# A new order table for a fused decay attention and gated MLP, with reciprocal transfers also issued by ScalarE

## The chip, the cores and the metric

The kernel runs on one core of a Trainium2 chip. The time is device microseconds of one execution. The core has TensorE (PE in the profile; PEld is its weight load), VectorE (DVE), ScalarE (ACT), GpSimd (POOL) and SyncE (SP), which here does nothing but issue transfers; each works through its own queue in order, and semaphores tie them together.

## What is computed

Inputs are q, k, v of 8 batches x 8 heads x 576 x 64, a forget factor f per position, a value weight and an output weight of 512 x 512, and a convolution weight of 5 x 512. Per head:

```python
scores = q @ k.T / sqrt(64)
cum = cumsum(log(clip(f, 1e-4, 1)))
scores = where(causal, scores + cum[i] - cum[j], -1e9)
attn = softmax(scores)          # sum + 1e-9 below the line
x = attn @ v
```

Then the heads of a batch are put side by side (x is 576 x 512) and

```python
gate = sigmoid(sum over k of conv_w[k] * x[s - 4 + k])
out = (gate * (x @ w_val)) @ w_out
```

## The kernel before

**Tiling.** Two heads make a pair; there are 32 pairs, four to a batch. Of a pair, TensorE computes scores in nine blocks (`plan_s`, class S; two pairs of heads, four row blocks and a joint tail). DVE adds the decay from a table in SBUF and finds the row maximum (line 479, class red), ScalarE takes the exponential with a row sum (line 483, class SX, tiles P and Pl). TensorE transposes the result (`plan_pt`, class PT, line 511) and ScalarE or DVE evicts the transposed blocks from PSUM to tile pt (line 268, class PE in the plan). TensorE multiplies with v (`plan_pv`, class PV), and DVE multiplies the product by the reciprocal of the row sums while evicting it (line 580, class X, tile x). The result is split into two fp32r halves, xh and its remainder xl (line 587), and is convolved: five products along the sequence, the first a plain product (line 273 on ScalarE, 275 on DVE or POOL), the other four on DVE (line 616); ScalarE's tanh makes the gate (line 592). After the fourth pair of a batch `plan_moe` computes x @ w_val (Mv), the gated product on DVE (line 648, H), its split (hh, hl) and the output product (Mo), whose eviction (ScalarE line 689, DVE line 691) halves it and whose store goes out in rows of 128. Pairs from the fifth on have their q and k split likewise into Xh and Xl (line 397 is Xl).

**The round trip of the reciprocals.** Row sums stand one per partition, but the product of PV needs them along the free dimension. So `rec` takes the reciprocals, TensorE transposes them with the last block (lines 529 and 530), they are copied to tile rt (line 532), written to DRAM with two transfers (class rzw, tile rzd, about 4.5 KB) and read back with two transfers that spread each row over 64 partitions of x32 (class rzr, 144 KB each). Line 580 uses them in place. A read may be issued when both writes have landed.

**Order.** Nothing is scheduled on the chip. The program first collects 2,712 pieces of work as nodes (`Plan.add`; `Plan.dma` adds a second node for the landing), each with the engines that may do it, what it reads and writes, and the PSUM banks that it is the first to touch. Then `Plan.order` reads TABLE: two characters give a node's number in base 64, a digit its engine (0 TensorE, 1 ScalarE, 2 DVE, 3 POOL, 4 SP), and a further digit each bank that it takes. Each engine gets its instructions in the order of the table; the table was found by a search outside the kernel. `load` makes a transfer; with `early=True` the table may give it to SP or ScalarE, otherwise only to SP. In the old table all transfers are on SP.

The issue itself is one line for all transfers (line 280):

```python
lambda e: (nc.sync if e == "SP" else nc.scalar).dma_start(out=out, in_=in_)
```

Of the kernel before, what the change touches and what calls it, by code (L numbers as in the profile page):

```python
# [47 lines left out]
423M15A41s21u14z21t24F24D23R003S11v35I37z44A14G14B24E14H0177t43A21y13x001z24M24C13y23D31A24-
023T034Y054143B13U13P063_44I21H45y449004U034Z11B24O23C31C14J14N13Q24K27v41D24L14P13E25_051E24T24t41G34a21S447016027K17L3482540475g24V15h25525845H31F15
647I13F26117B45e14d15f14W004X17J34b14c35S0135X21K24_11J15V25J046755T250025U15Z25118O45K25L18I48Q45O25P15Q252005R15a44e25M21M25c41L25313G25N11N11O27x45  # L50
Y15k077F382045W17H3832a345-16223H28X16b018Z38411P21Q11R37V0027G38-25l263036c16416f0646r18K46g15E46q26j46h4a147-
26p15i056s19X48W365071U18Y2670321468169015j25m21V29h047_15o16618026a17W27Y27X11X29i2bi47Z16l44f25n36d061W26e19j16n41Y18e008U3980734g2ba49d24h27M014651
Z28116v027R28f1aa1ab39e1ac1ad37S17T27U17N28M47O17P26t008c05992a938d17Q19Z47D48a0686018b28V39a16w21-
22038528716u26I05a7388068915p26x18i0278s18u1bg48v25q26y28j18m48_001649021_18g028t2942bo38k43I16J09119f26F076G09g19_46K2bp2bq3a839629518q4aw058h19719b2
9c19p029q18o46H26L1br1ax2ay1di48w049225r28y00231do45s29318x2an0724i1bc45t1ae06513as28z2ao29l009m1at16N04aq2af29k26z16O0aj28S4al2am1ah26M3ag16Q006R09n0
39t06ai1ap1bs3ex4au26S2dk4ak1dz36P2av19r056T2dq49u1be49s1242dA36V006W06U29o1dx3ar16Y046Z08C16A26B29x0179I1dw36X26-
29v056_18D29y19z49B49F49K1aI066C22629w1aE00aF19D4bL029H16D29L04aJ1bt065079J1bM2bN1bn3az2bC013bA26E1271bm3by2bz19N02bk4aA00bB1bH2bu2bv1bD2aG078A1bw2740
6aH1bx1dy3dm4bI1bE1aB2750a548E2aK00aL1aM075bF2703bP01bQ1aN1bJ2bK1ez4du37100720aZ19O2eF42522829M2bG1aQ4762aO4aS4292eM1aX2dT018B2dU2aC04aW1dV1aY12b3bT05
aU4bU1fM4aD27906732dv38F2dK034dL2dR2dB00521eD4dP2b0079P1dC2dM1dQ1eN3dI2dD1a-
03dJ1772bO2b_001783dE2dF1dG2bZ05dH1b12ca1cc1bV07bW19R3bX02dN2fO4eB4c022a1e301bR07c34a_2b43e41fU4fS4f-3dS1bS19S2g12cb1dX03b-  # L60
2c917a08G27b28H17e057f0b21c147c49T2c747j007k0eK3c54dY2eO1bY19Q2eP2f606eL3g239U2fY3b52eJ37g2b62cd03f_1f72dO1h74cf027l2eH4ds4f81cg2ce2b32ch1eZ045f42dW2c
i3eQ01620eT2f51g_4d_07e01eU1e-2cs03g03cj1e_1f02eX2h14cp07cq0ct0eY17h4eV2eW1f22cr2f31e7060b72eh1ej2j249V2h54e502e81e61fi04fj2f11hd3b82eR2dZ07cx06cy0d-
1eS1ck2cl27o02fQ4fZ3e94hg1hh3eb4ef4ed47p0gl04cA07cB0ei1e101ek2cu2fe00cv1cm2cn27q29W17r4en03gm2cw2gn1e21el04cC2cz2cD1b91fW4gc056em2ff1he1gf2gg1hf3kh4g3
02170jh1eo2fa04cE3fb1cF03gh2gd2gj27m4gk1hb3ga2gb1cG0cI04cJ0g42g51g62gi1cQ06jj3g82g91f92fm072ji3h34gp00cH2g71cK2ja4ge1fn2fc04fo4fz1fx2gq2fd1co1cL1fq4cM
3fk05fl2fw1gt01gu1fy2j44er2cR0hA03fs4cN02go2hB2kn4hC1hi00157cS2hc3hj2hr034fu4hl2fg06ky3fh1hm1hk1es2kw1hp2hn2hs2ho1hy2cO0fA06cP2cT2fC00ht1h94hu2fD2gB01
2gC1fB2gF4hw2gr05cU2hx1cV00gD4cW0gO2fG1kz2hq1kp4gx07hv1fE1gL2gN1fH2jk3gH4gM1cX2hM03c-
06c_0hz1et2eu2gs1fI2hD2ev2d02hO00gy1gz01gv04ep1gJ4hE02j84hN2gw1eq3gA1hI07hJ1hK06hG05hF2lw4kx2jg2jD03jE2gP07jF1hL2gR01gQ2hP1je3hH1fJ2gS2gV1j64ju024jv2e
w1jz2jA1jl06370kv3jw1jf3jB2cY4i201jm2hQ025kj4jc4kt3lE4jq2jn1d306d40kl4h_1js2jx2i12hR2jC1jy1fF2jo2kS04gT2jt1gW2lL3jr1d800jp1gX2hU4lN1kT2d90d51kU1jG2gU2
jP07jQ2i01h-
1i402hS4d14lC4hY4jT074jN05hW4i32i52i61i82jU2k32da1lK3k41ly4lO3k11k21mL4jO1kr4lM3m502m62fK2m71jV4kJ016kO2kK2oT4i73kA00475kP1mT4ku3kH2jL03kI1n03lI3jX4kQ  # L70
2kR1jZ4ie02if0j_4kF2kG1jM2d64ih05jJ07jK1mR4kM2kN1ig2kD2jH03gY2fL1jR02mN4db4ii0kB2kC1jS2kE1m-
2m_2dd07de0ij2jI1k503k700df1gZ2kL1kV2l6041li1mZ2n13lA4kW06lJ3l405l51mX3k-
02k_1lh1ik2il2i92ia2lj1k82lg1ip07l72l84la4ib2k62kb1iq0ir2nk00nl2oZ4ic2l005kY02o_4k91nm1lG4im07qe4qc4in0kX1kc2lP04301io2kZ1l12kd2lY067l205iu02iv0g-
1lS2lQ2lR1is2q64lU2m32m41dg4m12l32lZ2ix04iy0lV1lT1lW2lk05lm00m21lX1mf01it3l_2iz2m01iw2l-
1mh02p81p93le4ke2iA2m82mP4ml036mY3iB3mg1mb07lc4ka2m901mi1mv1mw2mj04mk1mm1mn4mp4mx2ln2ll2lo2lp3iC02iD0iF04id1iE2ma2mc1p61nb032p72my1n201675nc2lq1lr2md0
0me1n72ng2p52qn3n92mt4na1iG0iH2iP00ql3iI2iJ3n81ni2n32n41n52n61nd1nh1mr4ps04pt2mz07ne2pu1kf2kg1qm3mA2mB01mC2mD1no03mF2np2iQ0qo3oV4ls2mG2p33pj015po2nf1p
a06743iR1nj1rl4rC3nn2q84pk2rA1pf2nq00nr1iK02pb2pg1oX4nA040lt2nB2p43ph2mE3iL0nN1pc1mV4nC4qa4pl1pp1nL1iU06pd2nM1nw00pe1iM2pA01pm2iN4nK1nu02pq2mH2ns07pr1
pn1iS4lu2pi1nE4qj3sA4lv1rt4iV0qi3mI2rn4qk2pB1qH04qI2nx1qJ1py03nv1pv2nI4pw01nG4px2nt1rB3nQ00iW2mJ2pI021pz1pJ1ny04pK4pU1pS1pV2qp05376qu2pT1qy021mK1nz1sR
# [742 lines left out]
```

## Time and profile before

| | us |
|---|---|
| runs shown | 524.27, 532.27, 534.39 |
| their median | 532.27 |
| the profiled execution | 527.19 |
| its span, first to last instruction | 525.3 |

The profile is of one execution. Busy times are sums of the time in which an engine had an instruction in flight; for TensorE the ends are modelled and neighbours overlap. "Idle before" is the time that an engine stood before an instruction, put down to what came last. L253 is a helper that issues all products but the transposes, and L268 one that makes all copies, so there the tiles tell what it is: banks<-pt,vt is PV, banks<-xh,wall is Mv, banks<-wall,hh is Mo. P and Pl are what the exponentials write; "ACT P L483" as a releaser is that exponential. The clock was granted in full (the column PEclk, 1.00).

### The profile page before, as it was taken

Reading aid. Unit: us, or ns where it says so; the run is one execution under the profiler, and the core shown is the slowest. Engines: PE = TensorE matmul, PEld = TensorE weight load, DVE = VectorE, ACT = ScalarE, POOL = GpSimd, SP = SyncE. Lnnn points to the kernel's source line nnn. Section 1 sums busy time; section 2 is a strip of 40 time slices with the busy share of each in tenths; the row PEclk is TensorE's granted clock in tenths of the full one; section 3 lists DMA queues with packets and bytes.
Section 4 is the critical chain, followed back from the end, with each engine's and each line's share of the span. In section 5 each row is a group of like instructions: output and inputs, shape, how many; then the busy total and the mean of one; then the engine's idle time right before and its main releaser. Section 6 shows DMA issues by size and latency. Waiting matters only on the chain. (4 is left out here: it accounts for less than half of the span.)

```text
span 525.3 us, 12611 instructions
## 1 busy us (share of the span) xinstructions
PE 504.5 (96%) x4392; PEld 443.6 (84%) x4392; DVE 438.7 (84%) x1186; ACT 347.6 (66%) x991; POOL 224.3 (43%) x293
## 2 busy tenths in 40 slices
...
GB/s 212 307 237 325 282 282 288 187 225 157 224 214 136 233 238 190 154 247 198 213 202 271 126 262 219 235 178 225 205 243 259 204 157 144 121 69 2 22 81 100
DMA packets 35022, 103.39 MB, mean 197 GB/s; under 512 B 5072, under 2 KB 5328, under 8 KB 34960
## 3 DMA queue, kind: packets, MB, share of 16 engines
...
q8 instruction: 34, 0.56, 0.4%
...
## 5 line engine op out<-in xcount | busy, mean ns | idle before, releaser
L483 ACT ACTIVATE P<-banks,negm 128x128 f32<-128x128 f32 (+3 forms) x256 | 133.8, 532 | 38.4 <-DVE negm L479 35.5
L479 DVE CUSTOM_DVE_ANT_0 banks<-banks,dm 128x384 f32<-128x384 f32 (+3 forms) x256 | 120.5, 512 | 10.1 <-PE banks L253 6.6
L268 ACT COPY pt<-banks 128x256 f32<-128x256 f32 (+2 forms) x235 | 94.5, 437 | 41.7 <-PE banks L511 22.7
L253 PE MATMUL banks<-xh,wall 128*128 128x288 f32 x512 | 113.2, 300 | 0.0
L616 DVE SCALAR_TENSOR_TENSOR gate<-x,cw,gate 128x576 f32<-128x576 f32 x128 | 108.9, 857 | 1.1
L253 PE MATMUL banks<-pt,vt 128*64 128x128 f32 (+2 forms) x1408 | 95.8, 290 | 1.9 <-ACT P L483 1.9
L253 PEld LDWEIGHTS banks<-pt,vt 128*64 128x64 f32 x1408 | 84.0, 137 | 13.8 <-ACT P L483 3.1
L511 PE MATMUL banks<-ident,P 128*128 128x128 f32 x640 | 89.0, 277 | 5.5 <-ACT pt L268 2.5
L253 PE MATMUL banks<-wall,hh 128*128 128x512 f32 x288 | 91.9, 400 | 2.0 <-ACT P L483 0.9
L314 POOL TENSOR_SCALAR_AFFINE_SELECT dm<-dm 128x256 f32<-128x256 f32 x122 | 57.6, 498 | 84.0 <-DMA dm<-decd 66.9
L253 PEld LDWEIGHTS banks<-xh,wall 128*128 128x128 f32 x512 | 85.0, 188 | 1.3 <-DVE h L648 0.3
L511 PEld LDWEIGHTS banks<-ident,P 128*128 128x128 f32 x640 | 71.1, 140 | 15.3 <-ACT P L483 4.0
L253 PE MATMUL banks<-xl,wall 128*128 128x288 f32 x256 | 75.4, 295 | 0.0
L397 POOL TENSOR_TENSOR Xl<-Xr,Xh 128x576 fp32r<-128x576 f32 (+1 forms) x41 | 63.0, 1545 | 19.9 <-ACT Xh L268 16.0
L253 PE MATMUL banks<-Xh 128*128 128x288 f32 (+4 forms) x280 | 59.2, 339 | 3.7 <-ACT Pl L483 1.7
L253 PEld LDWEIGHTS banks<-wall,hh 128*128 128x128 f32 x288 | 51.2, 188 | 11.7 <-DVE x L580 1.4
L253 PE MATMUL banks<-wall,hl 128*128 128x512 f32 x144 | 56.4, 391 | 0.0
L253 PE MATMUL banks<-Xh,Xl 128*128 128x288 f32 (+4 forms) x280 | 54.8, 315 | 0.1
L253 PE MATMUL banks<-Xl,Xh 128*128 128x288 f32 (+4 forms) x280 | 54.0, 313 | 0.0
L483 ACT ACTIVATION_READ_ACCUMULATOR P<-banks,negm 128x1 f32 x256 | 52.6, 205 | 0.0
L253 PEld LDWEIGHTS banks<-xl,wall 128*128 128x128 f32 x256 | 48.2, 188 | 0.5
L587 POOL TENSOR_TENSOR xl<-x,xh 128x576 fp32r<-128x576 f32 x20 | 29.2, 1462 | 44.7 <-ACT xh L268 41.0
...
## 6 DMA issues: line engine op xcount, KB each, us to landing
...
```

The lines of the kernel that those rows point to most:

```text
L253: nc.tensor.matmul(out, lhsT=lhsT, rhs=rhs, start=start, stop=stop)
L268: (eng.copy if eng is nc.scalar else eng.tensor_copy)(out=out, in_=in_)
L314: nc.gpsimd.affine_select(out=t, in_=t, pattern=[[0, 2], [-1, P]], base=0, channel_multiplier=1, compare_op=ALU.is_ge, fill=-BIG)
L397: eng.tensor_tensor(out=Xl[r][:, a:e], in0=Xr[r][:, a:e], in1=Xh[r][:, a:e].bitcast(F32), op=ALU.subtract)
L479: nc.vector.tensor_tensor_reduce(out=sl, in0=sl, in1=add[:, o:o + ext], op0=ALU.add, op1=ALU.min, scale=-0.125, scalar=3.0e38, accum_out=n ...
L483: nc.scalar.activation(out=dst[:, o:o + ext], in_=bank(key)[:, c0:c0 + ext], func=AF.Exp, bias=negm[r][:, col], scale=-1.0, accum_out=zs[r ...
L511: nc.tensor.transpose(out=bank(key)[:, c:c + P], in_=Pt[m][:, BOFF[b] + P * j:BOFF[b] + P * j + P], identity=ident)
L587: any_("xl", {"POOL": 1.4, "DVE": 0.67}, p, lambda eng: eng.tensor_tensor(out=xl[s], in0=xv, in1=xh[s][:, :].bitcast(F32), op=ALU.subtract ...
L616: eng.scalar_tensor_tensor(out=gt, in0=src, scalar=wt_, in1=gt, op0=ALU.mult, op1=ALU.add)
```

## The change

TABLE is replaced as a whole: another order on each engine, another choice of engine where a node allows several, other PSUM banks. And the four transfers of the reciprocals' round trip may be issued by ScalarE. It was searched with transfers that are randomly late. No node is added or removed and TensorE's work is the same.

```diff
 TABLE = """
-0240040430s010w000c20u040e20f10740g10v030b30F40t010Q40520h20H10i20932g001240k12i00K20n20l10m10z32r0570C33342e30j10o43540I20J20E32h00q40630L10B32n22o12
+0710930430w000v010520040b30240e20F40t020I22e30H10K20f10h20Q40s010g10J22c40i20k20y30630L10M20N20D30A30j12g032562i00n10_40l12h03340C30m22r0743540q40O20o
...
-        load("rzw", 0.1, p + 0.03, rzd[i, :, 0:L0].rearrange("h (j q) -> h j q", q=P), rt[r][D:D + 2 * NB], [("rt", r)], [("rzd", i, 0)])
-        load("rzw", 0.1, p + 0.03, rzd[i, :, L0:], rt[r][D + 2 * NB:], [("rt", r)], [("rzd", i, 1)])
+        load("rzw", 0.1, p + 0.03, rzd[i, :, 0:L0].rearrange("h (j q) -> h j q", q=P), rt[r][D:D + 2 * NB], [("rt", r)], [("rzd", i, 0)], early=True)
+        load("rzw", 0.1, p + 0.03, rzd[i, :, L0:], rt[r][D + 2 * NB:], [("rt", r)], [("rzd", i, 1)], early=True)
         for h in range(2):
             load("rzr", 0.65, p + 0.04, x32[i % NXR][D * h:D * h + D, T0:], rzd[i, h:h + 1].to_broadcast([D, S]),
-                 [("rzd", i, 0), ("rzd", i, 1)], [("xb", i % NXR, h)])
+                 [("rzd", i, 0), ("rzd", i, 1)], [("xb", i % NXR, h)], early=True)
```

Read out of the two tables, the nodes per engine where they differ by more than two:

| work | before | after |
|---|---|---|
| first product of the convolution | DVE 11, ScalarE 13, POOL 8 | 2, 11, 19 |
| Xh | DVE 6, ScalarE 28, POOL 22 | 9, 24, 23 |
| Xl | DVE 15, POOL 41 | 22, 34 |
| xh | DVE 11, ScalarE 21 | 17, 15 |
| xl | DVE 12, POOL 20 | 9, 23 |
| hh | DVE 22, ScalarE 10 | 16, 16 |
| evictions of transposes | DVE 96, ScalarE 256 | 102, 250 |
| output eviction | DVE 16, ScalarE 20 | 7, 29 |
| add of tri to dl | DVE 10, POOL 22 | 6, 26 |
| writes of reciprocals (rzw) | SP 64 | SP 41, ScalarE 23 |
| reads of reciprocals (rzr) | SP 64 | SP 49, ScalarE 15 |

The first load of q and k is also ScalarE's in the new table. The reads on ScalarE are of pairs 3, 4, 5, 7, 14, 15, 17, 20, 22, 23, 25, 26, 28, 29 and 31, one each. Matmuls that the order puts between the copy to rt and the first use of the reciprocals: before 44 to 156, after 67 to 178.

## Rows read from the trace of the kernel before

**Rows 1.** The page's part 1: busy us, share of the span, instructions
```profile
PE 504.5 (96%) x4392; PEld 443.6 (84%) x4392; DVE 438.7 (84%) x1186; ACT 347.6 (66%) x991; POOL 224.3 (43%) x293
```

**Rows 2.** Stretches: us, busy us (instructions) of PE, PEld, DVE, ACT, POOL, clock, DMA, GB/s
```profile
0.00:79.00 79.00, 68.06 (x575) 52.73 (x577) 69.81 (x210) 70.21 (x193) 42.22 (x71) 1.00 0.86 274
79.00:500.00 421.00, 414.74 (x3709) 372.37 (x3706) 358.38 (x952) 273.86 (x794) 180.42 (x221) 1.00 0.58 189
500.00:525.30 25.30, 21.74 (x113) 18.50 (x111) 10.46 (x26) 3.56 (x6) 1.69 (x2) 0.98 0.22 82
```

**Rows 3.** What ended TensorE's idle time: us in total, times, longest us
```profile
PE banks L253 <- ACT P L483: 3.5, 3, 1.9
PE banks L511 <- ACT pt L268: 2.5, 3, 1.1
PE banks L511 <- ACT P L483: 2.1, 3, 1.2
...
PE banks L253 <- DVE x L580: 1.4, 4, 0.5
PE banks L371 <- POOL ident L323: 1.4, 1, 1.4
PE banks L253 <- DMA Xr<-in_x_dram: 1.2, 1, 1.2
```

**Rows 4.** The chain of waits that ended last: start us, us, what
```profile
483.45 0.27 ACT rt L268
...
484.38 1.70 DMA rzd<-rt
...
486.72 2.90 DMA x<-rzd
```

**Rows 5.** Timeline of TensorE and DVE: start us, us, instruction, idle before
```profile
155.55 0.44 PE L253 MATMUL banks<-Xh 64*128 64x384 f32 x2 [1.44 <-ACT Pl L483]
...
489.74 0.56 DVE L580 TENSOR_TENSOR x<-banks,x 128x384 f32<-128x384 f32 x1 [4.36 <-DMA x<-rzd]
...
491.34 0.73 PE L253 MATMUL banks<-wall,hh 128*128 128x512 f32 x2 [0.52 <-DVE x L580]
```

**Rows 6.** Groups by line: count, busy us, mean ns, idle before
```profile
L483 ACT ACTIVATE P<-banks,negm 128x128 f32<-128x128 f32 (+3 forms) x256 | 133.8, 532 | 38.4 <-DVE negm L479 35.5 <-PE banks L511 1.5 <-DVE Pl L490 0.3
...
L397 POOL TENSOR_TENSOR Xl<-Xr,Xh 128x576 fp32r<-128x576 f32 (+1 forms) x41 | 63.0, 1545 | 19.9 <-ACT Xh L268 16.0 <-DVE Xh L268 3.4
...
L268 ACT CAST xh<-x 128x576 fp32r<-128x576 f32 x21 | 14.1, 677 | 12.0 <-DVE x L580 12.0
L397 DVE TENSOR_TENSOR Xl<-Xr,Xh 128x640 fp32r<-128x640 f32 (+1 forms) x15 | 13.2, 879 | 1.2 <-ACT Xh L268 1.1
...
L689 ACT ACTIVATE ot<-banks 128x512 f32<-128x512 f32 x20 | 12.0, 600 | 26.3 <-PE banks L253 21.4 <-issue 3.6 <-DMA out_dram<-ot 1.3
...
L691 DVE TENSOR_SCALAR ot<-banks 128x512 f32<-128x512 f32 x16 | 10.9, 686 | 10.2 <-PE banks L253 5.4 <-DMA out_dram<-ot 4.6
...
L275 POOL TENSOR_SCALAR gate<-x,cw 128x576 f32<-128x576 f32 x8 | 7.6, 948 | 23.5 <-DVE x L580 22.2 <-issue 1.3
...
L275 DVE TENSOR_SCALAR gate<-x,cw 128x576 f32<-128x576 f32 x11 | 6.8, 614 | 0.1
L268 DVE CAST xh<-x 128x576 fp32r<-128x576 f32 x11 | 6.4, 585 | 0.2
```

**Rows 7.** Issues of tile rzd on SP's queue: ns min/median/max
```profile
L280 SPq DMA_DIRECT2D rzd<-rt x64: 597/626/697, 27.1 to 484.4; - x64
L280 SPq DMA_DIRECT2D x<-rzd x64: 444/496/1497, 30.6 to 486.7; - x64
```

**Rows 8.** What SP's queue waited for: us in total, times, longest us
```profile
SPq L280 <- DMA rzd<-rt: 35.1, 29, 4.9
```

More of the change, by code (lines that the diff above doesn't have):

```diff
@@ L48 @@
[L48 to L78, printed above, removed]
@@ new lines @@
+4J14N150010z34L11B24B21C13Q14U041z24C14F24O24P14t41A27z40B37v43D33E21D23N065_024G13O14T23U11E23F26028Q4540073B13C21F15515845h24V15f247063G25e11G36111S
+44Y047K35H34a25g15114W024-074X14_15S0034824d35J025171J18I44Z11K28O44b15V21L27I37J35Z25617H35-
+15Q25R17F31M252065315a41N15c45k045O25P15T25M25N15K25i075X27x48W31O25W15Y169038K47L21P25U167057D46d065L16e13H25E41Q162268182008X28Z26f0266q18-
+36g16j46p16s165056618Y28326b065j26r26h10x055l26a184163036417V0725o16c24e25m17W29h049i21R31U17X17-
+27G38029X49j18117M030167P2980457_17Q17N28e077O15n37R27T27Y27U1a148M44c36v004f28U39d24g26t03aa27S17Z18526n46l18a018V34h28c02a34ac31V28f11X2a938b18d1ab3
@@ new lines @@
+8S48i0678v18j18m48u188018918g028h18t29926w28s19e11Y16u26x19a15p29b28_0170294286038719519028k46y29Z46F066I041W2962911ad29p033I19716J06G01Z29q18o19f21-
+22039_49l009m1aw019228y03ax25q28w006K21_19g16H25r29319c19k29n065s2ay18q49t074i16L1ae042518x2a736M38z2ba4di4af29u1aj2bc4a83al2an007aq26N03br39o1au26O0d
+z16Q066R0ak1as29r056P2ag1bp19x034bs35t1ao2214ap16S26T29I2av1ar16Y066Z09J19s16z28C39H29K19y19z1bg4aE07ah2ai19v05aF29w1a54at1bm3bq26V04dx12312426W0be4bi
+46U36-
+2bo3bn39B46A2bL02aI006X2aJ19D19L07bt05064bM2bN16B2dk46C2do4bC0238A28B3am1az2dq46_19F4dy39N01by2bz1bu2bA2bJ2bv1aA06bK17405bH2bB1dA3bD2262ex49O2bE1750aB
@@ new lines @@
+1aM014bI17039M2bF2aN1bG16D2dm4bw2aW1aQ46E1271aK07eM1aL2bx17106aX2eF4720732762du3aZ2aO4dT02bP07bQ1aG04772fM4dw2aC06aY1dU2fU4252aU4aS47905dV1282292aH19R
+3aD1dK017dL2dB003247832b3dP2ez4dG2dC2eB4dQ1dv3bO2dM1b006b12eD4dD1dN2dE2a-
+01b_006a_22a17a0c92cb2dH1cc2bX02ca2bV01c018D2bR00dR2f_1c148E2dF18F27b17c4bT03fS4bY19P2dI2bZ06g13bk4fO4g02dX05b41c348G27j02c74bU1eO3b-
+1g22j24dY1eP2bW17k0dS1dJ1dO1dW2eN37l17e017f07g1f604cd03g_4c517h49Q29S29T2eL3f727m4bS1fY38H1f-39U2eJ3f81eK3b22ce2cf01cg2cj3ch1eQ02076eT2eZ045eU1e-
@@ new lines @@
+2e_1eV2d_03b33f42eW1ds4eR2eH47o017p0e300eS1f22f31eX2f02h14ci3e7072cs04ct0h54f51eY1ck2e817q1e01f11eh1cx01dZ03fi06b52cl2cp05cq0cm2e41ek29V29W1fj1cu2fQ4c
+y0b62hg1hh3ei1cn2eb4cr2e94ef4b72cv1e500ej1fe05e102e61ff1fZ3e21f92d-
+1cA04cB0ed4gl05gm2cw3el07cC2gn1cz2he1cD1co1j84en00fW4eo2em2gc035g302016gd2ge1gj2hf3hb3gk1fc07jj3er3cF04g82g91fd1fa01cG0gh2gi1ga2g42h74hd3gt07h34g62g51
+g71fk03fb2fm021fz1fx1b82b91gb1fn2fy1cI00cJ0jk3fl2ja4gp01gq1fq1gf2gg1fg06cN03cE3cH2fo4cQ01cK2cL2jh2cM2cO0cP2fw1fh1gu1hc3kh4hA04cR0hB2hC1cS2hr067fu4go2h
@@ new lines @@
+w2hx1ep2hs2hi01230kw1ht1fs4fC04hn2ji3lw4cT1hp2hq1hj2j44ho1hl2fA05hm1fD2fB2gB060gN1gx037r4gM1gO1hk1hI02cU2fG3hy2ky3gr04kp4gC2hu2hv1hJ2hM05cV00cW0hN1gL1
+c-
+06j64jD01gD4gF1gJ4gH4fH2gs1es2et2cX1fE2eu2je3hz1hO07gv05fF3gw2h94hK00jg3jf3gy1gz04c_0jE2gA1ju053gP04hD2lE4kn4jF1jz2kj4jB2lC4jC1jx2d01gQ2kx3kz3mL4hL1jy
+1gR02gS2jl01046js2hP1i203jq2jt1jr1jo2lL1hQ072hR1cY4jm2ev2jn1jv2hU4h_2i12h-
+2hS4jA1kl4hE06d304d40jp1kv3gT2fI2lK2eq3jw1jG2d51hG02hH1hW4hY4d800hF1lM2d14i01kS01i404gV3gW2ly4lN2lO2jJ07kT2kU1kr4fJ2jN06jO1jP02jQ1fK2jK2jc4gU2jT051k21
@@ new lines @@
+k41mT4jU1d64i52k31i32oT4k12jV4jL06jM1ku3d90da1m506m62i83i61o_4i72jX4m71j_4mR4kJ012kM2kt3kO2kA00534kQ2m-
+3kH2jH06jI1jZ4kD2kF2mN4kP1oZ4ie07if0kG1gX2ew1kE1db4kK2dd06de0kL1kN1ih05ii0gY2kB2kC1kW01i92n01kY00ia2ij2kR1ig2n12lA4gZ2kI1kV2m_3q64kX1l403k-
+02jR05jS1k_2fL1k707ik1k501df2k82l6025lj1l71l007l11la4lg1lh1ip04nk06mZ3iq0l84le4il2k62kb1l52li1g-
+1im05in0nl2nm1kZ1lI3ir2p53lJ3ib2ic2lP01324id1io2qc4lY006p81is2it3lU2l205lW2lX1lc4l31p61lZ2l-
+1lS2l_2mX3ix07m32lT1m41lG4dg4iy0lV1kc2m01lQ2m12p92iF05iG0mP4mY3iz2m21oV4iu04iv0kd2ke2lR1iw2iA1lk03ll2qe4lm02m82ml017mx1iB2iH2my1mm2mv1ln2mV4lo2md00me1
@@ new lines @@
+03q32td04x54tm2sZ1t41s407op06sk2q42sc4r_2w51uP3w63ok2ol2sg4oq0or2om01on0te1sK4sX1tc2s51vc03vd2uW00762rd1si4vU4oo2xd4uX2v-
+4re3sq05ve1uQ3vY4os1so01tf03u_2v01w73uY1rg2uZ2u-
+1ou04sp2sr2tg1xb4w83v12tp057su3vk06vl1ot3th00v21w23tC2tz2tq2tA1vg01vh2tB1uN4v3063v42wi027v62tt1wn2va2tj05v82tn01ov0ti1xk1tk1to1v71vb1tD00ow1rh2ri2v51w
+j2wk1xl2tF01v91vo03rj2vf2vs054wo1tr4w43tx4vp1tv4tG2vF1vE1sv2vt2wr01xm1vw1vW4xj3sw2ws2wt1vC1oz03tE2oA0tJ1yk4w906520vu1oB1ss2w33wp2vD1vq01wq1x74ox4xn3tH
+1As4oE04sx2yz3wa2wb1vi03wl2we2wf1tI3wm1wD06wg2wh1xh3st2vj1wv02ww1wc2oF0yA2wd1vr1sy2sz1vA4xG02tK2x94xH2xi3vm07vn2tL2w04tS00oG1tP01yB2oH4tM2oC4rk1tQ0q51
@@ new lines @@
+1AX2A_2u52BV3xR1BZ3y803B01y_04E94z707AY1D93AR1Da3BT3AS2vQ2yb2wZ1w-
+3y92AN1z01tO1z101z9020zk1zm2za1B504z22Bd06BL4Db3z82Dc2Bf01B61AT1zd1u91zj2ua2z300z41Be1ue03uf0ye3zl2zb4ug2zf1Cg04Ch2Ci1ub07yc1B42BU3CY4uc0ud2C7060Ca2C8
+2D04uh2Cb1B-03245Ce2C91Eq3C12Cf1Cc2C32Cd1oM4B_2C41zn07Bg1C01zp00zh4zo2Bh064D63Bi1Bb01Bt1AC4Gc4B907C52C61Ba1Co03Eh4C21Bs1zq2Ef4x12C-
+4ui2Bu1Cp2uj00Bl4x22uk0x32D83Bj4Bn4ul1zt1Dv03Bp4Br2Eo3Dw2uo02Bc1zu2zv2Dm016Dx1zr1Dn2Dd00534De2B707B81Dr2Df1Di2Ed4up0uq1ur4Cs07Eb4Ds1Ck00Cl1Dj1BR4En3Gk
@@ new lines @@
+2Gw2GZ05Gx1Gy2HH3CR2ER1Hv4EU07Gz1E02EV2GQ2zP02zQ0E-040zR2GW2F92E_1zy1Fb2II4uB4Fa2HJ3I006I12I21zS02zT0HE3G-
+1F82HT003Gm4zU2zV2zW3BF2BG1E31HK05124HP2HY2HN2HQ1HR2Ej4K14GR06HO1F04IV3z-07z_0A02GS1HS1zX02zY0HL2HM1EY07H1046HW2H-
+2H_1zZ2GT01H22G_02HU2EZ1IX3Fe05IS3IY3Hb1E11H51HZ1F24F44He2GU1Hd1Hc1HV1IW3F64Fc07J_4J6014HX1H01IK4A12A23IT3GX00E42GY1Fd2Ff2Fg1Ic07Id1I406E23I32Ig023A80
+0A90IO4IM4J72J81Jd2J92A307Fi3JX4Ja1Je1A40Jb2Jc1CS2I52CT2CU2IZ01564J42Ih1I-
+2HB4H34H71A51JV4H94Iq2J02Hh07Hi2J22JZ4K53Aa1Ab4Is1Ka3Kb3It2E52E62Hf00IQ4Ii1J11Ie02Fh3Ir1J31Hg2I807Fr03A64Hl3E72I92I_1Ik1Io4Fo05Fs0K81Jf00IU3Jg2Ft2Ai07
```

65 lines of the change are left out of this document (26 added, 39 removed).

## Prediction

> **What bounds the kernel now.** First the page's busy times: TensorE has matmuls in flight for 504.5 of 525.3 us, 96%, DVE 438.7 (84%), ScalarE 347.6 (66%) [rows 1]. No edit touches a matmul, so the first question is how much of the span is not matmul: 525.30 - 504.54 = 20.76 us. A busy TensorE is not one at its peak, but the instructions and their number stay, so I hold the 504.5 fixed.
>
> Next, where those 20.76 us lie [rows 2]. In the first 79 us TensorE misses 79.00 - 68.06 = 10.94 us; there DVE (69.81) and ScalarE (70.21) are both 88% busy, so this stretch has three engines near their limit. In the 421 us that follow it misses only 421.00 - 414.74 = 6.26 us, with ScalarE at 65% and DVE at 85%. At the end it misses 3.56 us, nearly all behind the last matmul.
>
> Then who ended TensorE's waits [rows 3]. ScalarE's exponentials and evictions do it most: 3.5 + 2.5 + 2.1 = 8.1 us. DVE's normalised x (line 580), which is what waits for the reciprocals from DRAM, ends only 1.4 us. 1.4 (the identity) and 1.2 (the first load) are the start and stay. So the movable idle is 20.76 - 1.4 - 1.2 - 3.56 = 14.6 us, 2.8% of the span: **that is the most that any order, engine choice or bank choice can win in an execution like the profiled one.**
>
> Last the round trip of the reciprocals, seen bare at the last pair [rows 4]: the copy to rt starts at 483.45, the write to DRAM runs 484.38 to 486.08, the read 486.72 to 489.62. That is 6.17 us from copy to landing. DVE stood 4.36 us for it, yet TensorE lost only 0.52 us at that place [rows 5], since other matmuls were queued.
>
> The profiled execution took 527.19 us: the span and 1.9 around it. The three runs shown are 524.27, 532.27 and 534.39, so it is 5.1 below their median, and executions of the old order spread over 10 us. That spread, not the idle of the profiled execution, is what an order against late transfers could aim at.
>
> **The change part by part.**
>
> *Engines.* I counted both tables by kind. The first product of a convolution goes from DVE 11, ScalarE 13, POOL 8 to 2, 11, 19. The remainder Xl goes from DVE 15, POOL 41 to 22, 34; the output eviction from DVE 16, ScalarE 20 to 7, 29; the cast xh from ScalarE 21, DVE 11 to 15, 17. Priced by [rows 6]: on DVE the convolution gives -9 x 0.614 = -5.5, Xl +7 x 0.879 = +6.2, the eviction -9 x 0.686 = -6.2, xh +6 x 0.585 = +3.5, together -2.0 us. On ScalarE the eviction gives +9 x 0.600 = +5.4, xh -6 x 0.677 = -4.1, the convolution (-2, at the eviction's price) -1.2: about 0. On POOL +11 x 0.948 - 7 x 1.545 = -0.4. The smaller shifts (hh, hl, xl, dl, evictions of transposes) are of that size and of both signs. DVE and ScalarE have over 80 us to spare each, so over the whole kernel I take 0.
>
> *The first 79 us* are where load could count. Ahead of the first 575 matmuls the new table has no cast Xh on ScalarE where the old has six, and three exponentials fewer; against that stand three more evictions, an xh and six DMA issues. Casts at xh's price: -6 x 0.677 + 0.677 = -3.4; exponentials -3 x 0.532 = -1.6; evictions at the output's price +3 x 0.600 = +1.8; issues about 6 x 0.6 = +3.6. That is +0.4 us of 70.2, so nothing by load, and DVE's count is the same within a microsecond. What is left is order: movable idle there is 10.94 - 2.6 = 8.3 us. The new table lets ScalarE issue the first load, but also puts a decode of conv_w, which waits for a load queued third on SP, ahead of the logarithm on ScalarE, and all decay tables hang on that logarithm. Bounds: all 8.3 us won, or as much again added. I take about a fifth won, -1.5.
>
> *Waits of the middle*, 6.26 us. The longest that I looked at is 1.44 us at 155.55, for a bank that an exponential had to free [rows 5]. They belong to one order, another order has others. I take a third won, -2, between all of it (-6) and as much again added (+6).
>
> *The round trip.* From the copy to rt to the first use, the old table lays 106 matmuls on average and at least 44 (the last pair; 49 at pair 11); the new one 116 and at least 67. The middle stretch runs 3709 matmuls in 421 us [rows 2], 0.1135 us each, so 6.17 us are 54 matmuls: two pairs of the old table have less cover than one bare round trip, none of the new. In the profiled execution it is worth little: -0.5, bounded by 0 and by -1.4, what line 580 costs TensorE [rows 3].
>
> *ScalarE as issuer.* 23 of 64 writes, 15 of 64 reads and one load move to ScalarE. On SP a write's issue held the queue 0.626 us and a read's 0.496 [rows 7]; ScalarE's own price is in no row, so I take SP's: 23 x 0.626 + 15 x 0.496 + 0.6 = 22.4 us more on ScalarE, 370 us in all, 70%. A read must first wait for both writes; on SP that wait came to 35.1 us over 29 cases, 4.9 at the longest [rows 8]. On ScalarE it would stop the exponentials and evictions behind it. For 10 of the 15 reads the table puts 18 or more matmuls (over 2 us) between write and read, longer than the bare write's 1.70 [rows 4]; for pairs 23, 26 and 28 none, for 5 and 17 ten and twelve. Cost between 0 (ScalarE idles a third of the middle) and 22.4 + 5 x 4.9 = 47 us; I take +0.5, near the lower end, since a 65% busy engine is the nearest row.
>
> *Banks* matter only through who frees them, which is inside the middle's waits.
>
> *Tail.* Both tables end with output products, an eviction on ScalarE and a store: 0. Between the last x and the first product that needs that head's gate the new table lays 114 matmuls, the old 132. In the old trace only 0.5 us was lost there [rows 5]; bounds 0 and 18 x 0.1135 = +2, taken 0.
>
> **Sum** against 527.19: -1.5 - 2 - 0.5 + 0.5 = -3.5, so 523.7 in an execution like the profiled one. The old runs' median lies 5.1 above its profiled execution. I give the new order's larger cover something, but no row shows which transfer was late in those runs: I add 2 instead of 5.1, and get **525.7 us**, 1.2% under 532.27. A measurement of this kernel can tell about 2% from no change, so this counts as the same. Its own range is 521 to 531.
>
> Does a transfer issued by ScalarE land sooner? SP's waits for the writes averaged 35.1 / 29 = 1.2 us, yet the longest was 4.9 [rows 8], against 1.70 for the whole bare write [rows 4]: something stood in its way, 3.2 us of it. The Trainium skill, "DMA: Bandwidth & Descriptors", speaks against a gain in its section "Issuing engines are not separate DMA queues": all issuers share the same 16 engines and only issue time is saved. By that the sum stays at 525.7, as it holds no faster landing. The same page's "Queues, rings and completion order" says that an engine takes turns between the issuers' queues packet by packet, by which a small transfer of ScalarE's would pass SP's large ones; with the late reads gone the 2 us for lateness would go, 523.7. No ScalarE-issued transfer is in this trace, so it shows neither.
>
> **The rivals.**
>
> *Nothing is won.* New waits replace the old one for one, and lateness hits as before: 527.2 + 5.1 = 532.3, or 528.8 with the -3.5. For it: TensorE is at 96%, and no row shows that it was the reciprocals that came late. Against: the shortest cover grows from 44 to 67 matmuls. This is also the case in which the change doesn't do what it says.
>
> *The order pays fully.* Two thirds of the 14.6 us of movable idle go and lateness is absorbed: 527.2 - 9.7 = 517.5. For it: the waits are many and small. Against: in the first 79 us the work of DVE and ScalarE does not shrink.
>
> *ScalarE blocks* (slower). Its in-order queue stops at the five close reads until the writes land, and the exponentials behind it come late for TensorE's transposes, which ScalarE already keeps waiting most. If TensorE pays half of 5 x 4.9 = 24.5 us (12.2) and a quarter of the issue time (5.6), it is 527.2 + 17.8 = 545.0. It decides where a read's wait exceeds the matmuls queued ahead of the next transposed block: the waits for line 483, now at most 1.9 us [rows 3], would come at 4 or 5. Against it: ScalarE's slack after 79 us.
>
> **Chances.** Forecast 0.55, nothing won 0.13, fully paid 0.22, ScalarE blocks 0.10. Under 521.6 (2% faster) lies the fully paid case: 0.22. Over 542.9 lies the blocked case: 0.10. The rest, 0.68, is within 2%. The range of 516 to 538 reaches down past the fully paid case and up past nothing won with a bad middle (532.3 + 6), and leaves out the blocked case.
>
> **What would show it.** Right: TensorE busy 503 to 506 us again, with 15 to 19 idle; ScalarE's waits on the writes short; DVE's wait for x at the last pair below 2 us; ScalarE's busy time within 5 us of 348; runs closer together than 10 us. Wrong: the same 575 first matmuls taking under 76 or over 82 us; TensorE waits of over 3 us behind line 483; or runs that still spread over 10 us, in which case lateness sits in other transfers than these.

## The result and the profile after

The new kernel takes 523.96 us (median of 20 runs) against 529.15 for the old one (20 runs): ratio 0.9916, 95% interval 0.9892 to 0.9939. It is 0.8% faster, beyond the noise, but counts as the same by the 2%. The prediction said 525.7 and "the same". The old runs span 524.27 to 534.39, the new ones 521.12 to 527.48; one of the 20 new runs, 621.67 us at a granted clock of 0.754, is left out of that spread. With 20 runs the old median is 529.15; the 532.27 of the first three runs stood 3.1 too high.

The profiled execution of after took 526.99 us (span 525.0), 3.0 above its median, where that of before lay 2.0 below its own. So the two profiles show hardly any difference in length, and are compared stage by stage. Two lines fewer stand above the code: L580 is now L578, L483 is L481, L253 is L251, L511 is L509, L268 is L266, L280 is L278. (In the experiments the table takes fewer lines again; the same six are L567, L470, L240, L498, L255 and L267 there, and in a_late, b_late, a_rz_late and b_rz_late one to five more.) The page's part 1 of after (engine, busy us, share, count):

```profile
PE 506.0 (96%) x4392; PEld 445.7 (85%) x4392; DVE 431.6 (82%) x1170; ACT 349.7 (67%) x992; POOL 231.5 (44%) x308
```

ScalarE gained 2.1 us of busy time against [rows 1] and DVE lost 7.1. The stretches of after, with the columns of [rows 2]:

```profile
0.00:79.00 79.00, 66.47 (x517) 50.36 (x517) 64.11 (x192) 62.92 (x174) 35.47 (x66) 0.96 0.78 247
79.00:500.00 421.00, 418.48 (x3763) 377.07 (x3762) 358.80 (x956) 283.54 (x813) 196.01 (x242) 1.00 0.60 196
500.00:525.30 25.30, 21.03 (x116) 18.29 (x114) 8.67 (x23) 3.26 (x6) 0.00 (x0) 0.96 0.17 62
```

TensorE's idle time between 79 and 500 us fell from 6.26 us [rows 2] to 421.00 - 418.48 = 2.52. But in the first 79 us it got through 517 matmuls instead of 575, and the granted clock was below full there (0.96): the records give half of it, 1.2 instead of 2.4 GHz, from 11.1 to 14.5 and from 62.3 to 65.7 us. The execution of before shows no such stretch until 524 us, and those of a_f_first, a_f_first_cw_late, a_sp_t and a_sp_t_f_first none until 519 us or later, so a part of this execution's late start is the clock's: at most half of those 6.8 us by my estimate, 3.4. What ended TensorE's idle time in after (engine, line, waited for: us in total, times, longest), as [rows 3]:

```profile
PE banks L369 <- POOL ident L321: 2.6, 1, 2.6
PE banks L251 <- DVE x L578: 2.3, 2, 1.6
PE banks L251 <- DVE gate L359: 2.1, 1, 2.1
PE banks L251 <- ACT pt L266: 1.9, 3, 0.7
...
PE banks L509 <- ACT P L481: 1.5, 3, 0.8
PE banks L251 <- ACT P L481: 0.7, 3, 0.3
PE banks L509 <- ACT pt L266: 0.6, 3, 0.3
```

ScalarE's exponentials (tile P) now end 2.2 us instead of 5.6 [rows 3]. The evicted blocks (pt) end 0.6 us instead of 2.5 before the transposes, but 1.9 instead of 0.2 before products, so by them nothing was won. Three waits of the start have come in: the identity (2.6 instead of 1.4), the first decay table (2.1) and one late x (1.6).

A window counted in matmuls, from the start of the 1000th (counted from 0) to the start of the last: first before, then after (columns of [rows 2]).

```profile
124.74:521.35 396.61, 390.35 (x3396) 349.00 (x3392) 328.31 (x869) 241.61 (x697) 155.40 (x191) 1.00 0.56 181
```
```profile
132.79:520.64 387.85, 387.04 (x3395) 348.75 (x3392) 318.53 (x847) 245.72 (x706) 166.56 (x205) 1.00 0.57 184
```

As many matmuls take 8.76 us less; they are nearly the same ones, since the order of TensorE differs by a few. Of it 6.26 - 0.81 = 5.45 is idle time and 3.3 is TensorE's own busy time, whose cause was not traced. In these two executions that gain of the middle is paid back at the start. The start of the nth matmul (counted from 0, so that 4391 is the last), in us, read from the traces of this study:

```
nth matmul            60    575   1000   2500   4391   1000 to 4391   575 to 4391
before              13.33  79.04 124.74 292.55 521.35   396.61         442.31
after               18.27  84.67 132.79 295.71 520.64   387.85         435.97
a_f_first           15.53  79.12 128.38 291.32 515.65   387.27         436.52
a_f_first_cw_late   15.65  81.79 130.62 294.31 518.62   388.00         436.83
a_sp_t              15.59  80.12 128.60 292.19 516.61   388.01         436.49
a_sp_t_f_first      15.20  78.28 127.05 290.83 515.14   388.08         436.85
a_sp                15.74  84.45 135.83 308.31 548.26   412.43         463.80
b_act_t2            13.55  82.61 129.22 300.23 530.04   400.82         447.43
```

The start of after, from the timeline (start us, us, what, idle before and what ended it):

```profile
0.81 1.21 SPq L278 DMA_DIRECT2D Pl<-in_f_dram  x2
0.84 0.40 ACTq L278 DMA_DIRECT2D Xr<-in_x_dram  x1
...
7.36 0.46 DVE L344 TENSOR_SCALAR Pl<-Pl 128x576 f32<-128x576 f32 x1 [5.82 <-DMA Pl<-in_f_dram]
7.45 0.22 ACT L703 ACTIVATE gate<-h 128x20 f32<-128x20 uint32 x1 [5.36 <-DMA h<-in_conv_w_dram]
7.85 0.68 ACT L346 ACTIVATE Pl<-Pl 128x576 f32<-128x576 f32 x1 [0.18 <-DVE Pl L344]
...
10.57 3.14 PE L251 MATMUL banks<-gate,dm 64*128 64x256 f32 x10 [2.10 <-DVE gate L359]
```

ScalarE issues the first load of Xr in the same moment as SP issues f. The small f, on which the decay tables hang, lands at 7.36; in the profile of before DVE started on it at 4.42. A little later TensorE waits 1.59 us for one x, and the chain of waits of after leads back from there to a transfer of vt and a write of reciprocals (start us, us, what):

```profile
42.75 7.61 DMA vt<-in_v_dram
...
50.44 6.70 DMA rzd<-rt
...
57.66 3.47 DMA x<-rzd
...
61.23 0.57 DVE x L578
```

A write of at most 4 KB took 6.70 us, where the bare one at the end of before took 1.70 [rows 4]. Behind that standstill lies the second stretch at half clock.

### The profile page after: what moved, and what is told of

It is laid out like the page before. It is cut to its first block, busy times and chain, and to the rows that moved or that the text cites. A ratio compares the mean times of both kernels' runs of the same rounds, so it can differ in the third digit from the quotient of the medians.

```text
span 525.0 us, 12616 instructions
## 1 busy us (share of the span) xinstructions
PE 506.0 (96%) x4392; PEld 445.7 (85%) x4392; DVE 431.6 (82%) x1170; ACT 349.7 (67%) x992; POOL 231.5 (44%) x308
## 4 chain that ended last, share of the span: by engine, by line
PE 78%; DMA 5%; DVE 5%; ACT 3%; issue 2%; SPq 0%; ACTq 0%; POOL 0%; DVEq 0%; POOLq 0%
PE banks L251 63%; PE banks L509 12%; PE banks L527 2%; DMA x<-rzd 2%; DVE banks L477 1%; DMA vt<-in_v_dram 1%; DMA rzd<-rt 1%; DMA dm<-decd 1%; ACT P L481 1%; DVE gate L614 1%; ACT pt L266 1%; DVE pt L266 1%; PE banks L528 1%; ACT Pl L481 1%; DVE h L646 0%
## 5 line engine op out<-in xcount | busy, mean ns | idle before, releaser
L481 ACT ACTIVATE P<-banks,negm 128x128 f32<-128x128 f32 (+3 forms) x256 | 133.6, 532 | 37.7 <-DVE negm L477 33.4
L266 ACT COPY pt<-banks 128x512 f32<-128x512 f32 (+2 forms) x228 | 92.7, 449 | 35.0 <-PE banks L509 17.3
L614 DVE SCALAR_TENSOR_TENSOR gate<-x,cw,gate 128x576 f32<-128x576 f32 x128 | 113.3, 893 | 2.0 <-POOL gate L273 0.9
L251 PE MATMUL banks<-xh,wall 128*128 128x288 f32 x512 | 112.6, 301 | 0.2 <-ACT P L481 0.2
L251 PE MATMUL banks<-pt,vt 128*64 128x128 f32 (+2 forms) x1408 | 95.6, 290 | 0.3 <-ACT P L481 0.3
L251 PEld LDWEIGHTS banks<-pt,vt 128*64 128x64 f32 x1408 | 83.8, 137 | 11.4 <-issue 2.8
L251 PE MATMUL banks<-wall,hh 128*128 128x512 f32 x288 | 92.0, 401 | 0.0
L509 PE MATMUL banks<-ident,P 128*128 128x128 f32 x640 | 88.7, 277 | 3.1 <-ACT P L481 1.5
L312 POOL TENSOR_SCALAR_AFFINE_SELECT dm<-dm 128x256 f32<-128x256 f32 x122 | 56.3, 485 | 71.0 <-DMA dm<-decd 59.4
L251 PEld LDWEIGHTS banks<-xh,wall 128*128 128x128 f32 x512 | 84.8, 188 | 0.9 <-ACT P L481 0.4
L509 PEld LDWEIGHTS banks<-ident,P 128*128 128x128 f32 x640 | 71.1, 140 | 12.3 <-ACT P L481 2.5
L251 PE MATMUL banks<-xl,wall 128*128 128x288 f32 x256 | 75.5, 295 | 0.0
L395 POOL TENSOR_TENSOR Xl<-Xr,Xh 128x640 fp32r<-128x640 f32 (+1 forms) x34 | 53.0, 1565 | 23.4 <-ACT Xh L266 15.0
L251 PE MATMUL banks<-Xh 128*128 128x288 f32 (+4 forms) x280 | 58.5, 340 | 4.5 <-DVE x L578 2.3
L251 PEld LDWEIGHTS banks<-wall,hh 128*128 128x128 f32 x288 | 51.5, 189 | 9.2
L251 PE MATMUL banks<-wall,hl 128*128 128x512 f32 x144 | 56.5, 393 | 0.0
L251 PE MATMUL banks<-Xh,Xl 128*128 128x288 f32 (+4 forms) x280 | 54.6, 318 | 0.0
L251 PE MATMUL banks<-Xl,Xh 128*128 128x288 f32 (+4 forms) x280 | 54.3, 317 | 0.0
L660 POOL TENSOR_TENSOR hl<-h,hh 128x576 fp32r<-128x576 f32 (+2 forms) x28 | 32.6, 1174 | 48.8 <-ACT hh L266 26.9
L481 ACT ACTIVATION_READ_ACCUMULATOR P<-banks,negm 128x1 f32 x256 | 52.5, 205 | 0.0
L251 PEld LDWEIGHTS banks<-xl,wall 128*128 128x128 f32 x256 | 48.2, 188 | 0.3
```

The source lines that it names most:

```text
L251: nc.tensor.matmul(out, lhsT=lhsT, rhs=rhs, start=start, stop=stop)
L266: (eng.copy if eng is nc.scalar else eng.tensor_copy)(out=out, in_=in_)
L312: nc.gpsimd.affine_select(out=t, in_=t, pattern=[[0, 2], [-1, P]], base=0, channel_multiplier=1, compare_op=ALU.is_ge, fill=-BIG)
L395: eng.tensor_tensor(out=Xl[r][:, a:e], in0=Xr[r][:, a:e], in1=Xh[r][:, a:e].bitcast(F32), op=ALU.subtract)
L481: nc.scalar.activation(out=dst[:, o:o + ext], in_=bank(key)[:, c0:c0 + ext], func=AF.Exp, bias=negm[r][:, col], scale=-1.0, accum_out=zs[r ...
L509: nc.tensor.transpose(out=bank(key)[:, c:c + P], in_=Pt[m][:, BOFF[b] + P * j:BOFF[b] + P * j + P], identity=ident)
```

## The experiments

Labels that begin with a_ start from the new table, those with b_ from the old one. "The 38" are the 23 writes and 15 reads of reciprocals that the new table gives to ScalarE. A time is the median of 6 to 12 runs. A ratio, with its 95% interval, is against runs of the old kernel beside it (medians 528.37 to 528.92 us); a difference in us is against 529.15 or 523.96.

### Who issues, and where in its queue

**a_sp.** All 38 entries get SP's digit; nothing else changes. One of them, a write of pair 28:

```diff
-H51
+H54
```

> The new table, with the 38 reciprocal transfers that it gives to ScalarE issued by SP at the same places of the order. Theory (the gain is the order's, ScalarE as issuer is worth nothing either way): 523 to 526 us, ratio to the kernel before 0.988 to 0.995, SP's waits for the writes up from 56 to about 80 us, TensorE's busy time unchanged. Rival (ScalarE as issuer is the gain, because SP's queue no longer stops for the writes): 527 to 530 us, ratio 0.997 or more, with TensorE waiting over 3 us for line 578.

Measured: 549.7 us, ratio 1.0409 [1.0363, 1.0454]. The theory fell. The rival's range of 527 to 530 us was far too low, though its sign came: TensorE waited over 3 us for x (line 578, here L567; below). **b_act** does the reverse with the old table: `early=True`, and the same 38 transfers get ScalarE's digit at their old places.

> The old table, with those same 38 transfers issued by ScalarE at their old places of the order. Theory (order, not issuer): within 2 us of the kernel before, ratio 0.996 to 1.006; possibly slower, since the old order puts several reads right behind their writes on ScalarE. Rival (the issuer is the gain): 524 to 526 us, ratio 0.995 or less.

Measured: 552.44 us, ratio 1.0427 [1.0373, 1.0482]; both fell again. In either kernel the reciprocals come late. DVE's waits for them (us in total, times, longest), in a_sp and then in b_act; after has 3.1, before 8.3:

```profile
DVE x L567 <- DMA x<-rzd: 21.4, 9, 6.1
```
```profile
DVE x L567 <- DMA x<-rzd: 23.0, 9, 5.1
```

In a_sp this reaches TensorE (after: 2.3 us in 2 waits). First what it waited in total, then the longest wait in the timeline, then two stretches from the clock's records (columns of [rows 2]):

```profile
PE banks L498 <- DVE x L567: 10.7, 4, 4.2
```
```profile
141.02 0.69 PE L498 MATMUL banks<-ident,P 128*128 128x128 f32 x2 [4.22 <-DVE x L567]
```
```profile
139.72:146.55 6.83, 5.53 (x14) 4.36 (x15) 6.14 (x21) 3.59 (x11) 3.51 (x3) 0.50 0.36 134
467.40:474.23 6.83, 6.44 (x26) 6.04 (x27) 5.72 (x9) 2.41 (x8) 5.56 (x6) 0.50 0.74 204
```

So a late x can be paid twice. TensorE stands, and around such a wait (from 136.8 to 141.0 us here) the granted clock falls to half, for 20.5 us of this execution in all.

Why does a change of issuer make them late? SP's queue in a_sp around pairs 27 and 28 (start us, us, what; an x3 is three issues, from the first's start to the last's end):

```profile
436.71 8.55 SPq L267 DMA_DIRECT2D rzd<-rt  x3
446.33 1.13 SPq L267 DMA_DIRECT2D x<-rzd  x2
```

The three are the first write of pair 27 (436.72), then H54, a write of pair 28 that has to wait for pair 28's rt (444.06), then the second write of pair 27 (444.72). Pair 27's reads stand behind all that. A place in the table is not a time: H51 stood ahead of F24, pair 27's second write, but in ScalarE's queue, where it held nobody of SP's.

**a_sp_t** tests this: also all 38 on SP, but SP's queue is sorted by the issue times in the trace of after. No transfer moves by more than five places in SP's queue, and the other engines' orders stay. The same spot of the table, transfers of pairs 27 and 28 only:

```diff
 F04
-H54
 F24
 F44
 F64
+H54
```

> The new order, engines and banks, with all 38 reciprocal transfers that ScalarE issues given to SP, each put into SP's queue at the place that its issue time in the trace of the new kernel gives it (it moves by at most five places against a_sp). Theory (the place in the in-order queue is what counts, not which engine issues): 523 to 527 us, like the new kernel, and DVE's waits for x<-rzd back at 3 to 5 us in the profile. Rival (SP alone cannot carry these transfers in the new order, because it stands up to 14 us behind output tiles): 535 us or more, with DVE's waits for x<-rzd above 10 us.

Measured: 522.67 us, ratio 0.9887 [0.9847, 0.9926]: the theory held, the rival fell. Its profile, first DVE's waits, then SP's queue at the same place:

```profile
DVE x L567 <- DMA x<-rzd: 4.1, 4, 1.8
```
```profile
415.82 1.29 SPq L267 DMA_DIRECT2D rzd<-rt  x2
420.10 1.55 SPq L267 DMA_DIRECT2D x<-rzd  x2
421.70 0.59 SPq L267 DMA_DIRECT2D dl<-decd  x1
423.13 0.59 SPq L267 DMA_DIRECT2D rzd<-rt  x1
```

Pair 27's two writes go out together, its reads 4.3 us after the first write instead of 9.6, and pair 28's write comes last. So the gain does not need ScalarE as issuer, and 27 us hang on places that differ by at most five. Of the 31.5 us between the spans of the two profiled executions (552.5 and 521.0), 19.1 are TensorE's idle time and 12.4 its busy time (515.2 against 502.8), in which the half clock lies. a_sp_t and the new kernel can't be told apart: their intervals overlap.

**b_act_t** was meant to do the same in the old table: the 38 on ScalarE, sorted by the issue times of before.

> The old order, engines and banks, with the same 38 transfers issued by ScalarE, each put into ScalarE's queue at the place that its issue time in the trace of the kernel before gives it. Theory (issuer alone is worth nothing; the gain is in the order): 527 to 531 us, like the kernel before. Rival (ScalarE as issuer is what wins): 523 to 526 us. A third (a transfer in ScalarE's queue waits for running work and delays TensorE's copies): 533 us or more.

Measured: 542.52 us, ratio 1.0263 [1.0222, 1.0304]. In it some reads of PSUM banks by ScalarE came to stand behind the bank's next user, so those parts of the computation read other data, and the time answers nothing. **b_act_t2** is the same with each bank's users in their old sequence.

> The old order, engines and banks, the 38 transfers issued by ScalarE at the place that their issue time in the trace of the kernel before gives them in ScalarE's queue; everything else stands in the old order, each PSUM bank with its old sequence of users. Theory (the issuer alone is worth nothing): 527 to 531 us. Rival (ScalarE as issuer is what wins): 523 to 526 us. A third (in the old order a transfer in ScalarE's queue stands behind that queue's waits, or holds its copies up): 533 us or more.

Measured: 534.54 us, ratio 1.0124 [1.008, 1.0169]. Sorting by time takes back 17.9 of b_act's us (552.44 to 534.54), and DVE's waits are 5.6 us. But the old order is 5.4 us slower (534.54 - 529.15) than with SP alone, above the theory's 531 and just in the third's range. TensorE's waits in b_act_t2:

```profile
PE banks L240 <- ACT P L470: 7.0, 5, 1.9
```

It was 3.5 us over 3 waits before [rows 3]. That ScalarE's exponentials come later behind the issues fits this row; no run takes that wait apart.

### The start

**a_f_first** gives the first load of Xr to SP, behind the two loads of f.

```diff
-071
...
 004
...
 024
+074
```

> The new table, with the first load of q and k given back to SP and put behind the two loads of f, as in the old table. Theory (the new start is slower because f shares the DMA engines with that load: f landed at 7.36 us instead of 4.42): f is in use by 4.6 us again, the first product with the decay table comes near 8 us instead of 10.57, the 60th matmul 2 to 4 us earlier, and the time falls by 2 to 3 us against the new kernel, to 521 or 522. Rival (the start is hidden, since DVE and ScalarE catch up by matmul 200, where the gap was 1.1 us): 523 to 525 us, as the new kernel.

Measured: 524.2 us, ratio 0.9907 [0.9877, 0.9937]. DVE's first row on f in its profile:

```profile
4.63 0.46 DVE L333 TENSOR_SCALAR Pl<-Pl 128x576 f32<-128x576 f32 x1 [3.10 <-DMA Pl<-in_f_dram]
```

f is back at 4.63, so the Xr load beside it was what delayed it by 2.7 us, and the 60th matmul starts 2.74 us sooner. The median is still that of the new kernel: the rival held.

**a_f_first_cw_late** also moves the decoding of conv_w behind the decay tables in ScalarE's and DVE's orders.

> The same, with the seven first steps of the decode of conv_w moved behind the decay tables on ScalarE and DVE, so that the logarithm waits for f alone. Theory: the logarithm starts at about 5.1 us as in the old kernel, 0.5 to 1 us more off the start than a_f_first, 520 to 522 us. Rival (the decode was off the path, its load landed with f): the same time as a_f_first within 0.5 us.

Measured: 524.72 us, ratio 0.9913 [0.9877, 0.9949]: nothing, as the rival had it. But the rival's reason is not what the traces show. The logarithm starts at 4.97 us against 6.57 in a_f_first, so the decode was in its way; the 60th matmul is no sooner for it (15.65 and 15.53). **a_sp_t_f_first** joins a_sp_t and a_f_first.

> a_sp_t with the first Xr load behind the two f loads on SP, as in a_f_first, so that no transfer at all is issued by ScalarE. Theory (the start is hidden by the waits that follow, as a_f_first showed): 522 to 524 us, as a_sp_t. Rival (with the reciprocals in place the start counts): 519 to 521.5 us, better than every kernel here.

Measured: 524.66 us, ratio 0.9924 [0.9894, 0.9953]. The rival fell, and with no transfer at all issued by ScalarE the time stays that of the new kernel. Two or three microseconds at the first table are gone before the end; where they go was not followed further.

### Lateness

**a_late** and **b_late** put a second transfer of the same row, to a spare place, ahead of each dm tile:

```diff
-            load("dec", 2.3 if i < 6 else 2.05, p + 0.05 * h, dm[m], decd[2 * i + h:2 * i + h + 1, 0:SW].to_broadcast([P, SW]), dk, [("dm", m)])
+            def twice(m=m, q=2 * i + h):
+                for to in (junk[q % 4], dm[m][:, 0:SW]):
+                    nc.sync.dma_start(out=to, in_=decd[q:q + 1, 0:SW].to_broadcast([P, SW]))
+            plan.dma("dec", {"SP": 0.57}, 2.3 if i < 6 else 2.05, p + 0.05 * h, lambda e, go=twice: go(), dk, [("dm", m)])
```

> The new kernel with each of its 60 loads of a dm tile preceded by a second transfer of the same row into a spare place in DRAM, which the output does not need: 60 x 655 kB more to move, so the reciprocals' transfers come later. Theory (the new order bears lateness better, its smallest cover being 67 matmuls where the old one has 44): at most 6 us above the new kernel, so up to 530 us. Rival (both orders are equally exposed): it loses as much as b_late does, within 2 us.

> The kernel before with the same 60 extra transfers. Theory: it loses more than the new order does, 8 to 15 us above the kernel before, so 537 to 544 us, with DVE's waits for x<-rzd above 12 us. Rival: it loses as much as a_late, within 2 us.

Measured: a_late 587.1 us, ratio 1.1101 [1.104, 1.1162]; b_late 601.87 us, ratio 1.1355 [1.1301, 1.1409]. The new order loses 63.1 us and the old one 72.7, so the sign is the theory's and the rival fell, but both sizes were off by far: this load makes everything late, not the reciprocals alone. POOL's wait for the dm tiles themselves, in a_late and then in b_late (59.4 in after and 66.9 in before):

```profile
POOL dm L305 <- DMA dm<-decd: 111.8, 32, 9.8
```
```profile
POOL dm L305 <- DMA dm<-decd: 155.5, 32, 21.4
```

So **a_rz_late** and **b_rz_late** delay the reciprocals alone, with half a pair of x (311 kB) ahead of each pair's first read, on the same issuer:

```diff
+            def behind(e, h=h):
+                q = nc.sync if e == "SP" else nc.scalar
+                if h == 0:
+                    q.dma_start(out=junk[i % 4], in_=x[i][:, 0:608])
+                q.dma_start(out=x32[i % NXR][D * h:D * h + D, T0:], in_=rzd[i, h:h + 1].to_broadcast([D, S]))
```

> The new kernel with one more transfer of 311 kB (half of the pair's x, to a spare place in DRAM, not needed by the output) ahead of each pair's first read x<-rzd on the same issuing engine, 32 in all. From a_late, where 60 transfers of twice the size took 119 us of all 16 DMA engines, one takes about 1 us; with its issue the reads come about 1.5 us, 13 matmuls, later. Theory (the smallest cover decides): no pair falls below the 54 + 13 matmuls, so 0 to 3 us above the new kernel, 524 to 527 us. Rival (both orders are equally exposed): it loses within 2 us of what b_rz_late loses.

> The kernel before with the same 32 transfers of 311 kB ahead of the reads x<-rzd. Theory: pairs 31, 11 and 0 with 44, 49 and 57 matmuls of cover fall 23, 18 and 10 matmuls short of 67, 5.8 us instead of 1.7 us, and with what follows from it 4 to 9 us above the kernel before, 533 to 538 us. Rival: it loses as much as a_rz_late, within 2 us.

Measured: a_rz_late 541.26 us, ratio 1.027 [1.0215, 1.0325]; b_rz_late 538.86 us, ratio 1.0214 [1.0161, 1.0268]. b_rz_late is just above its 533 to 538; a_rz_late loses 17.3 us where 0 to 3 were expected, more than the old order's 9.7. Both the theory and the rival fell. Stretches of a_rz_late, then of b_rz_late (columns of [rows 2]):

```profile
79.00:139.00 60.00, 53.26 (x483) 47.35 (x483) 45.37 (x125) 38.35 (x106) 29.16 (x37) 0.97 0.68 217
139.00:300.00 161.00, 155.33 (x1387) 140.61 (x1384) 132.02 (x357) 109.94 (x319) 70.74 (x89) 0.98 0.68 221
300.00:500.00 200.00, 197.49 (x1768) 176.99 (x1766) 165.92 (x451) 129.01 (x375) 94.61 (x114) 1.00 0.66 203
```
```profile
79.00:139.00 60.00, 58.70 (x546) 53.80 (x545) 53.66 (x145) 45.57 (x131) 32.22 (x38) 1.00 0.75 241
139.00:300.00 161.00, 157.32 (x1435) 140.48 (x1435) 136.70 (x379) 107.25 (x315) 70.54 (x92) 1.00 0.70 223
300.00:500.00 200.00, 195.78 (x1722) 173.50 (x1720) 164.94 (x429) 120.74 (x352) 77.42 (x95) 1.00 0.59 193
```

TensorE's idle time in the three stretches is 6.74, 5.67 and 2.51 us in a_rz_late, where after has 1.71, 0.03 and 0.78 in the same view: the delay adds 5.0, 5.6 and 1.7. In b_rz_late it is 1.30, 3.68 and 4.22, where before has 0.00, 2.95 and 3.31: it adds 1.3, 0.7 and 0.9. So the new order pays more in every stretch, and most of it before 300 us.

Three things fit that, and no run tells them apart. The first is the clock: a_rz_late's records have it at half for 13.7 us in all between 74 and 284 us, behind waits for x of 1.9 to 2.7 us, and b_rz_late's not before 533 us. The second is the covers. Counted as in the prediction, the small covers of the new order lie close together and early, where one late pair finds the next one short as well: pairs 6 and 7 have 82 and 68 matmuls (107 and 92 in the old order), pairs 10 and 11 have 82 and 67. And third, the 15 reads from ScalarE suffered more: 4.15 us from issue to the last packet (3.41 in after), those from SP 3.20 (3.00); the longest are those of pairs 3, 4, 5 and 7, 6.1 to 7.7 us. The threshold of 67 matmuls was too low in any case: from the later write's issue to the later read's issue after took 4.8 us on average over the 32 pairs, against 2.3 at the bare last pair of before [rows 4]. In before the average was 4.0, so in the new order a pair's read goes out later behind its writes, not sooner.

## Why the prediction was right, and where not

- **Bound.** TensorE was busy for 502.6 to 506.0 us in after and the four experiments of its speed, as said. No run here won more than the 14.6 us, but they no longer follow from the trace, since their premise was off. TensorE's busy time is not fixed: it was 515.2 us in a_sp, with the clock at half for 20.5 us, and about as many matmuls from the 1000th on took 3.3 us less of it in after than in before.
- **The sum, -3.5.** The lowest runs differ by 524.27 - 521.12 = 3.15 us, the medians by 5.2. The total came near by luck: the start was put too good, the rest too small, and the old median that it started from was 3.1 too high.
- **The first 79 us, -1.5: not won.** The 575th matmul starts 5.6 us later in after than in before, and 0.8 us sooner to 2.8 us later in the four experiments of its speed. The prediction's own sign of being wrong, the first 575 matmuls taking over 82 us, came in after with 84.67; up to 3.4 us of that are the clock's, as estimated above. Both things that the step named against it are in the trace: the first load issued by ScalarE, and the decode of conv_w ahead of the logarithm. Putting them right won nothing in the median.
- **Middle, -2, and round trip, -0.5: too small.** From the 575th matmul to the last the new order takes 436.0 to 436.9 us in five executions against 442.31 in the one of before, -5.5 to -6.3. These are the terms that were mis-sized, by a factor of more than two. The gain lies behind the 1000th matmul (-8.5 to -9.3); between the 575th and the 1000th 2.4 to 3.6 us are lost. It comes with the new table whoever issues. Which of its changed orders, engines and banks frees TensorE, no run separates.
- **ScalarE as issuer, +0.5: small, as said.** The same 38 transfers at the same moments from SP give 522.67, which can't be told from 523.96. ScalarE's busy time rose by 2.1 us, but issues are not counted in it; what they cost is in the last section. The blocked case was 0.10 and did not come. In the old table ScalarE as issuer did cost: 23 us in b_act, 5.4 at timed places. Only a part of it is that case's mechanism: in b_act TensorE waited longer for evicted blocks (7.1 us at L240 against 0.2) and for x, and no longer for the exponentials; in b_act_t2 it is the exponentials (7.0 against 3.5).
- **No sooner from ScalarE.** From a read's issue to its last packet it took 3.41 us (median of 15) from ScalarE and 3.00 (49) from SP in after; in the 15 pairs with one read of each, ScalarE's took 0.1 us longer at the median. This agrees with the Trainium skill, "DMA: Bandwidth & Descriptors", section "Issuing engines are not separate DMA queues". The small writes do not tell the issuers apart either: those of 4 KB took 1.66 us (10) from ScalarE and 1.68 (22) from SP, the longest 5.76 and 5.17. What the prediction drew from the Trainium skill, "DMA: Bandwidth & Descriptors", section "Queues, rings and completion order", a small transfer passing SP's large ones, does not show in these figures.
- **Lateness, +2 instead of 5.1.** The 5.1 came from a median of three runs; with 20 it is 2.0 above the profiled execution. The new runs lie within 6.4 us, the old ones within 10.1, but that the order did this is not shown: their standard deviations are 2.0 and 2.3 us, and the old kernel's runs beside the experiments lay within 6.1 to 8.5. Nor is it borne out that the larger smallest cover bears lateness: a_late speaks for it, a_rz_late against it.
